# Attention with one key head: values' products of two key steps in one stretch

## The chip, the cores and the metric

The kernel runs on one core of one Trainium2 chip. The metric is the device time of one execution in microseconds. The engines are PE (TensorE, matmul; its weight loads are shown apart as PEld), DVE (VectorE), ACT (ScalarE), POOL (GpSimd) and SP (SyncE, which here only issues DMAs). Matmul results go to PSUM, which the kernel uses as eight banks of 128 x 512 float32; ACT and DVE empty them.

## The reference

The input x is 2048 rows of 448. Two layers of the same shape follow each other, with the same weights:

```
x = x + A(layernorm(x))     # 16 query heads of 28, one key head and one value head
x = x + B(layernorm(x))     # h = sigmoid(x w_gate) * (x w_up), 1792 wide; h w_down
```

In A, q = x wq, k = x wk and v = x wv. For each head the scores q k^T / sqrt(28) go through a softmax over all 2048 keys, the result is multiplied with v, and the heads side by side are multiplied with wo. All heads share k and v. The inputs and outputs are float32.

## The kernel before, in words

**Tiling.** A layer has 16 *units* (`u`): 128 query rows with all 16 heads, as four groups of four heads. Each unit has 16 *steps* (`kt`) of 128 keys; a layer has 256 steps. In one step the kernel does for its 128 keys:

- four score matmuls `s` (line 584), one for each group of heads: keys as weights (96 x 128, three parts of the split key under each other), 512 query columns; each fills one PSUM bank, and ACT writes its exponential to a tile `P` (line 587), 128 x 512 float32;
- the values' products `pv` (lines 591 to 595): four matmuls, each with the values of these keys as 128 x 32 weights on its own 32 columns of the array (`tile_position=(0, 32 * g)`), from the four `P`; they are added up over the 16 steps in one bank of their own. A float32 matmul shows as two records, so a step's group shows as eight;
- the row maxima of a later unit, `mx` (line 549): four matmuls of 32 x 128 weights, each on its own 32 rows of the array, into four banks; DVE reduces each one (line 554). The softmax needs the maxima before the scores of that unit start. They go through a transpose `mt` (line 575), a copy on DVE and a DMA issued by POOL (line 578) into row 28 of the unit's queries `QS`;
- a share of *filler*: matmuls that belong to other work. This is the query projection `qp`, the output projection `wo`, and for every two units the gated layer: seven times gate `gp` and up `up` (44 matmuls of 256 columns each time, chains of line 352), then `dn` (line 784). ACT and DVE make `th` and `h` between them (lines 746 to 758).

**Order.** The kernel is scheduled by hand: each engine does its instructions in the order in which the code records them. In every step a string of letters sets this order:

```
ORDER = "FSFSFSFSPXM"
```

S is one score matmul with its exponential, F one slice of filler, P the values' products of the step before, M one step of maxima (four matmuls, four reductions), X the bookkeeping: `tick()` runs the side stages of finished units (DMAs of the sums, reciprocal, output, layer norm, transposes), each due a number of ticks after the one before. The first 48 steps of the second layer use another string (`LATER`) in steps after a step with maxima. `fill.slice(ns)` lets the filler generators run until their estimated cost has used up `ns`; `rate` spreads what is left over the steps that remain. At the start of a slice, `flush()` records the instructions on ACT and DVE that were put off since the last one.

**Banks and buffers.** One PSUM bank holds `pv`. The seven others share one tag `f`: scores, maxima, and the filler's results. A new tile takes a bank that was given back earlier, and PE waits until its last reader is done. `P` tiles rotate in 8 buffers of 2 KB a partition.

Of the kernel before, what the change touches and what calls it, by code (L numbers as in the profile page):

```python
# [8 lines left out]
F32 = mybir.dt.float32  # L9
# [10 lines left out]
def interleaved_layers_kernel(ctx: ExitStack, tc: tile.TileContext, x, wq, wk, wv, wo, wg, wu, wd, out, layers=2):  # L20
# [6 lines left out]
    nc = tc.nc  # L27
    _, S, D = x.shape
    F = wg.shape[1]
    H, Dh = 16, 28  # L30
    NT, NB, G, KT, FC = S // 128, S // 512, H // 4, S // 128, F // 128
# [10 lines left out]
    wk1 = ctx.enter_context(tc.tile_pool(name="wk1", bufs=2))  # L42
# [27 lines left out]
    def flush(every=False):  # L70
        todo, pend[:] = pend[:], []
        for i, (due, fn) in enumerate(todo):
            if due > now[0] and not every:
                pend.append((due, fn))
            else:
                fn()
        if every and pend:
            flush(True)
# [89 lines left out]
    def prep_b():  # L168

        NPG, FIRST = 7, 8  # L170
        mall = wk1.tile([128, 3, NPG], F32, name="mall", bufs=1)
# [43 lines left out]
        def pieces(a, z, ahead):  # L215
            for n in range(a, z):
                r = get()
                squares(mall[:, n // NPG, n % NPG:n % NPG + 1], r, r)
                fetch(min(ahead, z - n - 1))
                yield  # L220
        yield from pieces(0, FIRST, 5)
        parts = wk1.tile([128, 2], F32, name="parto", bufs=1)
# [14 lines left out]

        yield from pieces(FIRST, 3 * NPG, 4)
        todo += [(columns, f) for f in range(FC)] + [(rows, f) for f in range(0, FC, 2)]
# [125 lines left out]
    def layer_tiles(l):  # L365
        KK[l] = lay.tile([128, 2, S], F16, tag="KK", name="KK")
        VV[l] = lay.tile([128, KT, 32], F32, tag="VV", name="VV")
        nc.vector.memset(VV[l][:, :, 28:32], 0.0)
        nc.vector.memset(VV[l][:, :, 28:29], 1.0)
# [55 lines left out]
    def qgen(l, b):  # L425

        XT = XTQ.pop((l, b))
        for g in range(G):
            yield from qproj(l, XT, b, g)
        flush(True)  # L430
# [7 lines left out]
    def load_qs(l, u):  # L438
        b, t = divmod(u, 4)
        assert QDONE[l, b] == G  # L440
        q = wk1.tile([96, G, 4, 128], F16, name="QS", bufs=2)
        QS[l, u] = q
        for i, part in ((0, 0), (1, 0), (2, 1)):
            for g in range(G):
                nc.sync.dma_start(q[32 * i:32 * i + 32, g],
                                  qd[l % 2][b, g, part, :, t * 128:(t + 1) * 128].rearrange("(h d) n -> d h n", d=32))
# [38 lines left out]
    def soon(u, kz):  # L485

        return (u == 0 or u in AHEAD) and kz <= S - 512
# [93 lines left out]
    def scores(l, u, kt, g, P):  # L581
        assert ("m", l, u) in stored, (l, u, kt)
        s = psf.tile([128, 512], F32, tag=BANKS["s"], name="s", bufs=NBK[BANKS["s"]])
        nc.tensor.matmul(s, KK[l][0:96, 0, kt * 128:(kt + 1) * 128], QS[l, u][:, g].rearrange("p h n -> p (h n)"),  # L584
                         start=True, stop=True)
        p = wk1.tile([128, 512], F32, tag="P", name="P", bufs=8)
        nc.scalar.activation(p, s, AF.Exp, scale=esc)  # L587
        P.append(p)

    def pv(l, u, kt, P):  # L590
        if kt == 0:
            PVS[l, u] = psv.tile([128, 512], F32, tag="v", name="pv")
        v = PVS[l, u]
        for g in range(4):
            nc.tensor.matmul(v[32 * g:32 * g + 32], VV[l][:, kt], P[g], start=kt == 0, stop=kt == KT - 1,  # L595
                             tile_position=(0, 32 * g))
        if kt == KT - 1:
            o = wk1.tile([128, 512], F32, name="pvs", bufs=1)
            nc.scalar.copy(o, v)
            PVS[l, u] = o  # L600
# [5 lines left out]
    def later(*stages):  # L606

        side.append([stages[0][0], list(stages)])
# [276 lines left out]
    fill = Filler()  # L885
# [7 lines left out]
    xr0 = {}  # L893

    def load_x0(i, eng=nc.sync):
        if i < HB:
            xr0[i] = wk1.tile([128, D], F32, tag="h", name="xr0", bufs=HB)
        else:
            xr0[i] = wk1.tile([128, D], F32, tag="P", name="xr0", bufs=8)
        eng.dma_start(xr0[i], x[0, i * 128:(i + 1) * 128])  # L900

    hl0, ls0 = {}, {}
    for i in range(NT):
        load_x0(i)
        if i == 1:
            load4(rkv[:, 0], wk)
            load4(rkv[:, 1], wv, nc.gpsimd)
        if i == 3:
            load4(rq, wq)
# [127 lines left out]
    ORDER = "FSFSFSFSPXM"  # L1037
    MORE = (10,)
    HEAD = U * KT - 32
    sparse = ()  # L1040
    LATER = "FSFSFSPFSXM"
    FIRST = KT * TB + 17
    KEEP = 28000
    VS = 1800
    for l in range(layers):
        mx = mxs[l]
        final = l + 1 == layers
        while late:
            late.pop(0)[1]()
        if not l:  # L1050
            mx.step()
            fill.slice(0.4 * QCH)
            mx.step()
        else:
            mx.todo.sort()
            n = sum(a[0] < 4 for a in mx.todo) + 2
            sparse = [i * (3 * KT - 1) // n for i in range(n)]
        if not final:
            layer_tiles(l + 1)
        if l:  # L1060
            for b in range(2, NB):
                fill.add(qgen(l, b), G * QCH)
        flush(True)
        fill.slice((0.75 if l else 0.4) * QCH)
        prevP = None
        rate = 0.0
        for step in range(U * KT):
            u, kt = divmod(step, KT)
            if step == HEAD and not final:
                mxs[l + 1] = Maxima(l + 1)  # L1070
            P = []
            for o in LATER if l and step < 3 * KT and step - 1 in sparse else ORDER:
                if o == "S":
                    scores(l, u, kt, len(P), P)
                elif o == "M":
                    if l and step < 3 * KT:
                        n = step in sparse
                    else:
                        n = 1 + (u == 0 and kt in MORE)
                    if not n:  # L1080
                        mx.visit()
                    for _ in range(n):
                        if not mx.step() and not final and l + 1 in mxs:
                            a = mxs[l + 1].between()
                            if a and soon(a[0], mxs[l + 1].need(a)):
                                mxs[l + 1].step(a)
                    if kt == 5 and u + 1 < U:
                        load_qs(l, u + 1)
                elif o == "P":
                    if prevP is not None:  # L1090
                        pv(*prevP)
                elif o == "X":
                    if u and kt == 1:
                        b = (u - 1) // TB
                        if (l, b) not in BLK:
                            BLK[l, b] = Block(l, b)
                        later(*BLK[l, b].tile(u - 1))
                    if l == 0:
                        paced(step)
                    tick()  # L1100
                    fed = sum(BLK[l, b].fed == TB for b in range(NBL) if (l, b) in BLK)
                    if fed < NBL - 1:
                        rate = fill.left / max(FIRST + TB * KT * fed - step, 1)
                    else:
                        rate = max(fill.left - KEEP, 0) / (U * KT - step)
                else:
                    fill.slice(rate / ORDER.count("F"))
            prevP = (l, u, kt, P)
        pv(*prevP)
        flush(True)  # L1110
        later(*BLK[l, NBL - 1].tile(U - 1))
        n = 0
        nx = None if final else mxs[l + 1]
        while side or pend or (fill.gens if final else not nx.started()):
            tick()
            for _ in range(0 if fine else 4):
                fill.slice(VS / 4)
            n += 1
            a = None if final else nx.between()
            if a:  # L1120
                kz = nx.need(a)
                if soon(a[0], kz):
                    go = n >= 2 and not fine
                elif kz == S - 128:
                    go = len(fine) > 1
                else:
                    go = True
                if go:
                    nx.step(a)
                    n = 0  # L1130
            for _ in range(2 if fine else 0):
                fill.slice(VS / 4)
        if not final:
            fill.slice(QCH)
# [21 lines left out]
```

## Time and profile before

| | us |
|---|---|
| median of three runs | 2310.68 |
| lowest, highest | 2307.3, 2311.08 |
| the profiled execution's own time | 2311.88 |
| its span | 2310.1 |
| PE busy | 2237.5 (97%) |
| DVE busy | 1640.6 (71%) |
| ACT busy | 1584.3 (69%) |
| POOL busy | 336.9 (15%) |

The first scores of layer 0's fifth unit start at 321.4 us and its last at 1129.0; layer 1 has its scores from 1247.4 to 2215.0, from its fourth unit on from 1381.7. A row of the grouped view names the line, the engine, the operation, the tiles (output<-inputs) and their shapes, the count, and then the busy time, the mean duration in ns, and the idle time of the engine just before with what ended it. A row of the stretches gives begin and end, the length, and the busy time with the count for PE, PEld, DVE, ACT and POOL, then PE's granted clock, the share of the DMA engines, and GB/s. A row of the timeline gives the start and the length from the first start to the last end, the engine, the line, and the count of equal instructions in a row. The ends of matmuls are modelled, so distances are taken from start to start. A row of the waits names who waited for whom, the time in all, the times and the longest.

### The profile page before, as it was taken

Reading aid. Unit: us, or ns where it says so; the run is one execution under the profiler, and the core shown is the slowest. Engines: PE = TensorE matmul, PEld = TensorE weight load, DVE = VectorE, ACT = ScalarE, POOL = GpSimd, SP = SyncE. Lnnn points to the kernel's source line nnn. Section 1 sums busy time; section 2 is a strip of 40 time slices with the busy share of each in tenths; the row PEclk is TensorE's granted clock in tenths of the full one; section 3 lists DMA queues with packets and bytes.
Section 4 is the critical chain, followed back from the end, with each engine's and each line's share of the span. In section 5 each row is a group of like instructions: output and inputs, shape, how many; then the busy total and the mean of one; then the engine's idle time right before and its main releaser. Section 6 shows DMA issues by size and latency. Waiting matters only on the chain.

```text
span 2310.1 us, 41518 instructions
## 1 busy us (share of the span) xinstructions
PE 2237.5 (97%) x15915; PEld 1011.2 (44%) x15915; DVE 1640.6 (71%) x2905; ACT 1584.3 (69%) x2595; POOL 336.9 (15%) x590
## 2 busy tenths in 40 slices
PE   7998999999999999999998999999999999999999
PEld 3322343444444444444563224444444444444456
DVE  7888887777777777777885447777777777777322
ACT  5797786677767677776514997777676767767731
POOL 5014771101110110101001010000000000000010
PEclk9999999999999999999999999999999999999999
DMA  4333661423313132332341123233232313233233
GB/s 137 105 101 96 205 218 41 110 74 96 114 55 105 43 111 71 96 103 74 106 133 38 31 59 106 69 91 91 83 89 54 105 42 108 65 91 88 76 100 116
DMA packets 203623, 213.28 MB, mean 92 GB/s; under 512 B 135377, under 2 KB 164241, under 8 KB 203425
## 3 DMA queue, kind: packets, MB, share of 16 engines
q1 hardware_dynamic: 198080, 195.78, 28.8%
q0 software_dynamic: 5344, 14.87, 1.8%
q8 instruction: 124, 2.03, 0.4%
q14 instruction: 75, 0.61, 0.1%
HBM read 175.37 MB, written 23.59 MB: 86 GB/s over the span
## 4 chain that ended last, share of the span: by engine, by line
PE 58%; DVE 3%; ACT 2%; DMA 1%; issue 1%; POOL 0%; SPq 0%; DVEq 0%; ACTq 0%; POOLq 0%
PE pv L595 13%; PE s L584 12%; PE dn L784 8%; PE up L352 8%; PE gp L352 8%; PE mx L549 4%; PE wo L695 2%; DVE mp L554 2%; ACT P L587 1%; PE qp L352 1%; DMA wgu<-wgu_d 1%; DVE th L754 0%; DMA XT<-hl 0%; DVE oT L676 0%; PE kv L352 0%
## 5 line engine op out<-in xcount | busy, mean ns | idle before, releaser
L587 ACT ACTIVATE P<-s,esc 128x512 f32<-128x512 f32 x2048 | 1323.8, 690 | 447.4 <-PE s L584 420.5
L554 DVE TENSOR_REDUCE mp<-mx 128x1 f32<-128x512 f32 x2048 | 1269.7, 683 | 426.3 <-PE mx L549 424.1
L584 PE MATMUL s<-QS,KK 96*128 96x512 f16 x2048 | 764.2, 382 | 39.2 <-DVE mp L554 15.0
L352 PEld LDWEIGHTS <-wgu 128*128 128x128 f16 x4928 | 458.2, 97 | 237.8 <-issue 93.9
L595 PE MATMUL pv<-P,VV 128*32 128x512 f32 x4096 | 548.2, 607 | 0.0
L352 PE MATMUL gp<-XT,wgu 128*128 128x256 f16 x2464 | 374.4, 273 | 0.1
L352 PE MATMUL up<-XT,wgu 128*128 128x256 f16 x2464 | 373.9, 273 | 0.4 <-ACT P L587 0.3
L784 PE MATMUL dn<-WD,h 128*128 128x448 f16 x1344 | 321.4, 352 | 0.0
L584 PEld LDWEIGHTS <-KK 96*128 96x128 f16 x2048 | 197.4, 97 | 155.9 <-issue 59.8
L549 PEld LDWEIGHTS <-QH 32*128 32x128 f16 x1792 | 45.8, 91 | 350.4 <-issue 347.9
L549 PE MATMUL mx<-KK,QH 32*128 32x512 f16 x1792 | 186.5, 386 | 6.1 <-ACT P L587 3.1
L784 PEld LDWEIGHTS <-h 128*128 128x128 f16 x1344 | 123.8, 97 | 137.4 <-issue 25.7
L595 PEld LDWEIGHTS pv<-P,VV 128*32 128x32 f32 x4096 | 81.0, 108 | 199.6 <-issue 196.5
L757 ACT ACTIVATE h<-th 128x512 f16<-128x512 f32 x112 | 70.3, 628 | 110.1 <-DVE th L754 109.8
L669 POOL TENSOR_TENSOR lb<-pvs,lb 128x512 f32<-128x512 f32 x32 | 41.4, 1294 | 604.8 <-DMA lb<-sums 499.2
L306 POOL TENSOR_SCALAR rs<-mv 128x1 f32<-128x1 f32 (+1 forms) x50 | 12.1, 241 | 781.7 <-DVE mv L291 738.2
L352 PE MATMUL qp<-XT,WQ 128*128 128x512 f16 x352 | 115.9, 387 | 0.7 <-ACT P L587 0.4
L754 DVE SCALAR_TENSOR_TENSOR th<-th,up 128x512 f32<-128x512 f32 x112 | 76.1, 680 | 38.8 <-PE up L352 32.2
L758 DVE SCALAR_TENSOR_TENSOR h<-th,h 128x512 f16<-128x512 f32 x112 | 77.6, 693 | 36.0 <-ACT h L757 36.0
L746 ACT ACTIVATE th<-gp,gsc 128x512 f32<-128x512 f32 x112 | 76.7, 685 | 37.8 <-PE gp L352 37.8
L695 PE MATMUL wo<-WO,oT 128*128 128x448 f16 x384 | 95.1, 359 | 5.0 <-ACT oT L675 4.6
L352 PEld LDWEIGHTS <-WQ 128*128 128x128 f16 x352 | 33.4, 98 | 59.8 <-issue 34.2
(151 smaller groups left out, 916.9 us busy)
## 6 DMA issues: line engine op xcount, KB each, us to landing
wgu<-wgu_d SPq DMA_DIRECT2D x224, 512.0 KB
QS<-qd SPq DMA_DIRECT2D x384, 32.0 KB
lb<-sums SPq DMA_DIRECT2D x128, 64.0 KB
xr<-in_A_x_dram SPq DMA_DIRECT2D x32, 224.0 KB
qd<-qst POOLq DMA_DIRECT2D x28, 256.0 KB, 2.7
wgu_d<-sgu POOLq DMA_DIRECT2D x14, 512.0 KB, 4.1
x2d<-x SPq DMA_DIRECT2D x16, 224.0 KB
xr<-x2d SPq DMA_DIRECT2D x16, 224.0 KB
```

The source lines that it names most:

```text
L352: nc.tensor.matmul(ps, a, b, start=n == 0, stop=n == 10)
L549: nc.tensor.matmul(ps[h][:, i * w:(i + 1) * w], qh[32 * h:32 * h + 32, g], KK[l][32 * h:32 * h + 32, 1, ka:kz], start=True, stop=True, til ...
L554: nc.vector.tensor_reduce(o, ps[h].rearrange("p (g k) -> p g k", g=n), axis=AX.X, op=OP.max)
L584: nc.tensor.matmul(s, KK[l][0:96, 0, kt * 128:(kt + 1) * 128], QS[l, u][:, g].rearrange("p h n -> p (h n)"), start=True, stop=True)
L587: nc.scalar.activation(p, s, AF.Exp, scale=esc)
L595: nc.tensor.matmul(v[32 * g:32 * g + 32], VV[l][:, kt], P[g], start=kt == 0, stop=kt == KT - 1, tile_position=(0, 32 * g))
L695: nc.tensor.matmul(p, v["oT"][:, a, h * 128:(h + 1) * 128], WO[:, c, h], start=n == 0, stop=n == 11)
L746: defer(lambda: nc.scalar.activation(th, gp.rearrange("p j n -> p (j n)"), AF.Tanh, scale=gsc))
L754: nc.vector.scalar_tensor_tensor(t, th, 1.0, up.rearrange("p j n -> p (j n)"), op0=OP.add, op1=OP.mult)
L757: nc.scalar.activation(h[:, 0], t, AF.Copy, scale=2.0 ** -17)
L758: defer(lambda: nc.vector.scalar_tensor_tensor(h[:, 1], t, 2.0 ** -17, h[:, 0], op0=OP.mult, op1=OP.subtract), 1)
L784: nc.tensor.matmul(p, hs[f // 2][:, a, o:o + 128], WD[:, f, c], start=n == 0, stop=n == 3 * FC - 1)
```

## The change

In layer 0 from the fifth unit (`u > 3`) and in layer 1 from the fourth (`u > 2`), 400 of the 512 steps, a step's order depends on whether its number in the unit is even or odd. An even step has two letters P at its end, an odd step has none, and each P now takes one waiting step: so an even step does the values' products of the last two steps, one group right after the other. The odd step has its first two scores together, the even step its last two. Per pair of steps there are seven slices of filler instead of eight, and the share of a slice is set accordingly. X stands earlier in both strings. Before these units the order is as it was; `LATER` only concerns the first three units of layer 1, so it stays in use there.

`P` has 12 buffers instead of 8, and the first load of x, which uses the same tag, names the same number. The descriptor scratch that the program sets aside for DMAs issued by POOL is set to 8192 bytes a partition, which makes room for the four buffers.

```diff
-        p = wk1.tile([128, 512], F32, tag="P", name="P", bufs=8)
+        p = wk1.tile([128, 512], F32, tag="P", name="P", bufs=12)
...
+    PAIR = ("FSFSXFSSPPM", "FSSFSXFSFM")
...
-        prevP = None
+        waiting = []
...
-            for o in LATER if l and step < 3 * KT and step - 1 in sparse else ORDER:
+            paired = (l or u > 3) and u > 2
+            if paired:
+                order = PAIR[kt % 2]
+            else:
+                order = LATER if l and step < 3 * KT and step - 1 in sparse else ORDER
+            for o in order:
...
                 elif o == "P":
-                    if prevP is not None:
-                        pv(*prevP)
+                    for _ in range(len(waiting) if not paired else min(1, len(waiting))):
+                        pv(*waiting.pop(0))
...
-                    fill.slice(rate / ORDER.count("F"))
-            prevP = (l, u, kt, P)
-        pv(*prevP)
+                    fill.slice(2 * rate / (PAIR[0] + PAIR[1]).count("F") if paired else rate / ORDER.count("F"))
+            waiting.append((l, u, kt, P))
+        while waiting:
+            pv(*waiting.pop(0))
...
-    nc = _bacc.Bacc("TRN2", target_bir_lowering=False, num_devices=1)
+    nc = _bacc.Bacc("TRN2", target_bir_lowering=False, num_devices=1, dynamic_dma_scratch_size=8192)
```

PE at the end of a step in layer 1, before (the `x4` are four products, eight records of the profile):

```order
L584 LDWEIGHTS KK
L584 MATMUL s<-QS,KK 128x512
L595 MATMUL pv<-P,VV 32x512 x4
L549 LDWEIGHTS QH
L549 MATMUL mx<-KK,QH 128x512
```

The same place of an even step in the changed kernel:

```order
L584 LDWEIGHTS KK
L584 MATMUL s<-QS,KK 128x512
L584 LDWEIGHTS KK
L584 MATMUL s<-QS,KK 128x512
L595 MATMUL pv<-P,VV 32x512 x8
L549 LDWEIGHTS QH
L549 MATMUL mx<-KK,QH 128x512
```

Two scores stand together, and two groups of products follow without anything between. In the whole program the products stand in 312 stretches instead of 511.

PE at the end of an odd step in layer 1 in the changed kernel, where the filler is the up projection (of each kind of matmul one with its weight load):

```order
L584 LDWEIGHTS KK
L584 MATMUL s<-QS,KK 128x512
L352 LDWEIGHTS wgu
L352 MATMUL up<-XT_18534,wgu 128x256
L549 LDWEIGHTS QH
L549 MATMUL mx<-KK,QH 128x512
```

Where the products stood, there is now a slice of filler, and the maxima follow it. That is so in 225 places of the program instead of 58.

ACT in layer 1 in the changed kernel, through the exponentials of an even step (first four rows), of the odd step behind it (the next four exponentials) and the next even step's first:

```order
L587 ACTIVATE P_19444<-s_19442,esc_100 128x512
L587 ACTIVATE P_19452<-s_19450,esc_100 128x512
L587 ACTIVATE P_19462<-s_19460,esc_100 128x512
L587 ACTIVATE P_19466<-s_19464,esc_100 128x512
L587 ACTIVATE P_19495<-s_19493,esc_100 128x512
L587 ACTIVATE P_19499<-s_19497,esc_100 128x512
L746 ACTIVATE th_19501<-gp_19415,gsc_101 128x512
L587 ACTIVATE P_19510<-s_19508,esc_100 128x512
L587 ACTIVATE P_19519<-s_19517,esc_100 128x512
L587 ACTIVATE P_19543<-s_19541,esc_100 128x512
```

The tanh of the gate, recorded at the start of the odd step's second slice, stands between the second and the third exponential of that step. In the 200 odd steps this place holds another ACT instruction 33 times, the place between the third and the fourth 62 times.

More of the change, by code (lines that the diff above doesn't have):

```diff
@@ L898, in load_x0 @@
         else:
-            xr0[i] = wk1.tile([128, D], F32, tag="P", name="xr0", bufs=8)
+            xr0[i] = wk1.tile([128, D], F32, tag="P", name="xr0", bufs=12)
         eng.dma_start(xr0[i], x[0, i * 128:(i + 1) * 128])
```

## The prediction

> **What bounds the kernel now.** I read the page first (busy shares and slices), then the two stretches that the change touches, then the waits of PE in them, then the timeline of single steps.
>
> ```profile
> PE 2237.5 (97%) x15915; PEld 1011.2 (44%) x15915; DVE 1640.6 (71%) x2905; ACT 1584.3 (69%) x2595; POOL 336.9 (15%) x590
> PE   7998999999999999999998999999999999999999
> PE pv L595 13%; PE s L584 12%; PE dn L784 8%; PE up L352 8%; PE gp L352 8%; PE mx L549 4%; PE wo L695 2%; DVE mp L554 2%; ACT P L587 1%; PE qp L352 1%; DMA wgu<-wgu_d 1%; DVE th L754 0%; DMA XT<-hl 0%; DVE oT L676 0%; PE kv L352 0%
> L587 ACT ACTIVATE P<-s,esc 128x512 f32<-128x512 f32 x2048 | 1323.8, 690 | 447.4 <-PE s L584 420.5
> L595 PE MATMUL pv<-P,VV 128*32 128x512 f32 x4096 | 548.2, 607 | 0.0
> 321.40:1129.00 807.60, 792.38 (x5769) 363.86 (x5766) 608.56 (x1067) 574.84 (x922) 101.91 (x215) 1.00 0.30 87
> 1381.70:2150.00 768.30, 762.64 (x5509) 347.50 (x5507) 567.02 (x968) 551.19 (x870) 55.78 (x121) 1.00 0.28 82
> ```
>
> The last two rows are layer 0 from its fifth unit and layer 1 from its fourth: PE is busy for 792.38 of 807.60 us and 762.64 of 768.30 us, at a granted clock of 1.00. ACT and DVE have a quarter free, and what they miss is mostly PE's output. So what shortens PE's own row shortens the run, unless a new wait of PE eats it. PE's waits there are small today:
>
> ```profile
> PE s L584 <- DVE mp L554: 2.1, 6, 0.5
> PE s L584 <- ACT P L587: 2.1, 5, 0.4
> PE wo L695 <- ACT P L587: 0.5, 1, 0.5
> ...
> PE s L584 <- ACT P L587: 7.7, 9, 3.1
> PE s L584 <- DVE mp L554: 3.4, 13, 0.5
> PE mx L549 <- ACT P L587: 3.1, 4, 0.9
> ```
>
> The first three rows are layer 1, the others layer 0: 4.7 and 14.2 us, together 18.9, of waits for a PSUM bank that ACT (exponentials) or DVE (maxima) still reads.
>
> **What a stretch of values' products costs beside its arithmetic.** Start times on PE in one step:
>
> ```profile
> 1507.84 0.38 PE L584 MATMUL s<-QS,KK 96*128 96x512 f16 x1
> 1508.15 1.06 PE L595 MATMUL pv<-P,VV 128*32 128x512 f32 x8
> 1509.15 0.39 PE L549 MATMUL mx<-KK,QH 32*128 32x512 f16 x4
> 1509.47 0.55 PE L784 MATMUL dn<-WD,h 128*128 128x448 f16 x2
> 1509.86 0.38 PE L584 MATMUL s<-QS,KK 96*128 96x512 f16 x1
> 1510.08 0.73 PE L784 MATMUL dn<-WD,h 128*128 128x448 f16 x3
> 1510.65 0.38 PE L584 MATMUL s<-QS,KK 96*128 96x512 f16 x1
> ```
>
> A score ahead of dn takes 0.22 us (1509.86 to 1510.08), ahead of pv 0.31: entering pv costs 0.09. From pv to mx it is 1.00 us. The trace has one place where two pv groups already stand together, at the end of layer 1:
>
> ```profile
> 2215.03 0.38 PE L584 MATMUL s<-QS,KK 96*128 96x512 f16 x1
> 2215.34 1.92 PE L595 MATMUL pv<-P,VV 128*32 128x512 f32 x16
> 2217.20 0.61 PE L352 MATMUL gp<-XT,wgu 128*128 128x256 f16 x4
> ```
>
> Sixteen records take 1.86 us where two times eight take 2.00: a joint stretch saves 0.14 beside one entry of 0.09.
>
> The loss is that the odd step's maxima no longer follow pv but filler. At the layer change they do so already:
>
> ```profile
> 1151.98 3.77 PE L784 MATMUL dn<-WD,h 128*128 128x448 f16 x19
> 1155.69 0.39 PE L549 MATMUL mx<-KK,QHB 32*128 32x512 f16 x4
> ```
>
> Nineteen dn at 0.19 each (0.57 for three above) are 3.61, and mx starts after 3.71: entering mx from filler costs 0.10.
>
> **The sum of the sure part.** Counted in the two orders: 199 stretches of pv fewer, 167 entries into mx from other work than pv more, and in 11 pairs the transpose mt, which followed pv, now follows filler.
>
> ```profile
> 1503.73 1.06 PE L595 MATMUL pv<-P,VV 128*32 128x512 f32 x8
> ...
> 1504.61 0.22 PE L575 MATMUL mt<-id,m 128*16 128x128 f16 x1
> ```
>
> There pv took 0.88 instead of 1.00, so those 11 lose 0.12 and, at pv's price, an entry of 0.09. 199 x (0.09 + 0.14) = 45.8; less 167 x 0.10 = 16.7; less 11 x 0.21 = 2.3: PE's row gets **26.8 us** shorter. The number of matmuls is the same, and filler moves only between slots: seven slices a pair instead of eight.
>
> **What the new order may cost.** Each tile of scores or maxima takes the bank of an earlier one, and the odd step is now short. I lay it out for the gate and up phase, where steps are shortest.
>
> ```profile
> 1464.06 0.38 PE L584 MATMUL s<-QS,KK 96*128 96x512 f16 x1
> 1464.48 2.66 ACT L587 ACTIVATE P<-s,esc 128x512 f32<-128x512 f32 x4 [1.10 <-PE s L584]
> 1467.34 0.40 PE L549 MATMUL mx<-KK,QH 32*128 32x512 f16 x4
> 1467.76 2.48 DVE L554 TENSOR_REDUCE mp<-mx 128x1 f32<-128x512 f32 x4 [0.97 <-PE mx L549]
> 1468.34 0.60 PE L352 MATMUL gp<-XT,wgu 128*128 128x256 f16 x4
> 1468.60 0.69 ACT L587 ACTIVATE P<-s,esc 128x512 f32<-128x512 f32 x1 [1.45 <-PE s L584]
> 1468.77 0.38 PE L584 MATMUL s<-QS,KK 96*128 96x512 f16 x1
> 1469.18 0.62 ACT L757 ACTIVATE h<-th 128x512 f16<-128x512 f32 x1
> 1469.70 1.26 ACT L587 ACTIVATE P<-s,esc 128x512 f32<-128x512 f32 x2
> ...
> 1567.36 2.42 ACT L587 ACTIVATE P<-s,esc 128x512 f32<-128x512 f32 x4
> ```
>
> ACT and DVE start 0.42 after the score or the maxima. Exponentials in a row come every 0.58 ((2.42 - 0.69) / 3), an ACT instruction between two adds 0.52 (1469.18 to 1469.70), and the reductions come every 0.60 ((2.48 - 0.68) / 3). A slice of filler is four matmuls in 0.43 today (1468.34 to 1468.77) or three; with seven slots for the same work I take 0.46. In an odd step, counted from its first score: third score 0.90, fourth 1.58, maxima 2.36 (0.10 of entry in it), next even step's first score 3.15 (0.33 of maxima, 0.46 of filler later). The four exponentials end at 1.11, 1.69, 2.27, 2.85. In the order the fourth maxima tile takes the third score's bank in 107 of 200 odd steps: margin 0.09. The next first score takes the fourth's in 77: margin 0.30. With nothing between, no wait.
>
> With something between: in 33 odd steps an ACT instruction (tanh, h, a copy) stands between second and third exponential, and the maxima wait 0.52 - 0.09 = 0.43 in 107/200 of them, else the next score 0.22 in 77/200: 33 x 0.27 = 9 us. In 62 it stands between third and fourth: 62 x 0.22 x 0.39 = 5 us. On DVE the even step's reductions are over 0.75 before the odd step's begin (between the two maxima lie 0.33 of maxima, 0.46 of filler and 2.36, together 3.15; less 4 x 0.60). In 68 odd steps two or more instructions stand between, which makes the next four about 0.45 late; a later score that takes a maxima bank then waits some 0.13 on average: 9 us. New waits: 23 us. Against that the place of today's bank waits goes: the second score of an odd step took a bank of the maxima just before it in a third of the pairs, now in an eighth; I take half of today's 18.9 off, 10 us. **Net 13 us.** Bounds: from below, no new wait and 10 gone (-10); from above, every one of the 107 tight maxima waiting the 0.43 (46 us), with the other 14 (60 us), and none of today's gone. The rows have slack left in the bare step, so I stay near the lower third.
>
> **What I cost at nothing.** P has twelve buffers because three steps of four are alive; the first buffer is asked for again one step after its pv, so ACT's write is covered. The side stages come earlier in a step, and their ticks are alternately longer and shorter; POOL's product and ACT's cast are the pair that could block ACT:
>
> ```profile
> L675 ACT CAST oT<-lb 128x512 f16<-128x512 f32 x32 | 19.7, 616 | 8.4 <-POOL lb L669 8.4
> ...
> 1505.40 0.62 POOL L578 DMA_DIRECT2D QS<-mr  x1 [8.63 <-DVE mr L577]
> ...
> DMA to landing us min/median/max: 1.6/2.1/5.2
> ```
>
> The cast waits 8.4 us in all today, and its tick gets the longer half. The row of maxima for the next unit is issued at 1505.40, 4.46 us ahead of that unit's first score (1509.86), and lands in 2.1: of 2.3 us to spare the short odd step takes about 0.5. If the smaller descriptor scratch held POOL's transfers back, this is where it would show; 25 units at up to 0.5 us, 12 us, is its upper end. I take zero.
>
> **The sum.** The profiled execution took 2311.9 us (span 2310.1). 2311.9 - 26.8 + 13 = 2298; it lies 1.2 above the median of the runs, so I predict **2297 us**. Its own range is 2288 to 2308.
>
> **Rivals.**
> - *The whole gain arrives.* If the waits stay at today's level: 2310.7 - 26.8 = 2284 (2279 to 2288). For it: the bare odd step has no wait by the rows, and the even step leaves ACT and DVE two us of pv to catch up. Against: margins of 0.09 and 0.30 below one ACT instruction.
> - *The odd step's banks decide (slower).* If the fourth maxima and the scores behind them wait on average 0.20 us a pair more than today, that is 200 x 0.20 = 40: 2310.7 - 26.8 + 40 = 2324. It decides from 0.13 us a pair on (26.8 / 200). For it: ACT needs 2.85 of 3.15 us there; a backlog brought in from the even step hits every pair. Against: the order puts two scores first, and both engines idle a quarter. The Trainium skill, "TensorEngine Tiling (Array Packing)", PSUM Bottleneck, warns that packing speeds TensorE up but not the emptying of PSUM; today's 18.9 us of such waits agree in kind, not in size.
> - *The seam is not free.* If the second group pays its head again in mid-kernel, the 0.14 and so 199 x 0.14 = 27.9 us go: 2310.7 + 1.1 + 13 = 2325. Against it stands the row of sixteen, but that is one place. The Trainium skill, "TensorE: Matmul & The Clock Gate", The mechanism, says that a weight load overlaps running matmuls only where the row group differs, which would make this the outcome; the row of 1.86 disagrees.
>
> **How the numbers follow.** Forecast 0.50, whole gain 0.26, banks 0.16, seam 0.05, something else 0.03. From no change a measurement can tell about 0.2%, 4.6 us. Faster by more: the whole gain and nine tenths of the forecast, 0.72. Slower by more: most of banks and seam, 0.16. Within: 0.12. For eight in ten I leave out the ends of the whole gain below 2280 and of the slower cases above 2318.
>
> **What would show it.** pv in stretches of sixteen with 1.86 us to the next start; filler to mx 0.10; PE busy time about 27 us less. The waits of PE on ACT and DVE should sum to about 32 us in the two stretches, with mx on ACT the new row. If mx and s wait over 45 us, I am wrong on the price of the odd step; if the pv stretch takes 2.00, on the seam; if a unit's first score waits for the maxima's row, on the scratch.

## The result, and the profile after

| us | before | changed |
|---|---|---|
| median | 2310.88 (4 runs, 2307.3 to 2311.99) | 2288.85 (4 runs, 2284.06 to 2289.33) |
| profiled execution, span | 2311.88, 2310.1 | 2284.06, 2282.3 |

The ratio is 0.9904 (95% interval 0.9888 to 0.992): 22 us faster. The time lies in the predicted range, and 8 us under the predicted 2297. The profiled execution of the changed kernel is the lowest of its four runs; the same kernel measured a second time (below) gave 0.9922 (0.9909 to 0.9935).

From the page of the changed kernel, the engines, PE's slices and the three groups that the change touches on PE:

```profile
PE 2213.4 (97%) x15915; PEld 1030.0 (45%) x15915; DVE 1638.6 (72%) x2905; ACT 1545.7 (68%) x2595; POOL 338.1 (15%) x590
PE   8998999999999999999999999999999999999989
L584 PE MATMUL s<-QS,KK 96*128 96x512 f16 x2048 | 699.3, 380 | 29.7 <-DVE mp L554 12.0
L595 PE MATMUL pv<-P,VV 128*32 128x512 f32 x4096 | 506.0, 602 | 0.6 <-ACT pvs L599 0.6
L549 PE MATMUL mx<-KK,QH 32*128 32x512 f16 x1792 | 188.4, 385 | 3.3 <-DVE mp L554 2.2
```

The scores' row before:

```profile
L584 PE MATMUL s<-QS,KK 96*128 96x512 f16 x2048 | 764.2, 382 | 39.2 <-DVE mp L554 15.0 <-ACT P L587 14.8 <-DMA QS<-mr 4.1
```

PE is busy 24.1 us less with as many instructions, and the products' group fell from 548.2 to 506.0. The scores' group fell by more, but that is no gain by itself: two scores that stand together overlap in the modelled ends (0.60 for two in the timeline below, 0.38 for one), and 400 such neighbours make up the difference. Where the time went shows in the stretches. First before, then changed: layer 0 from its fifth unit, the change of layers, and layer 1 from its fourth unit to its last score:

```profile
321.40:1129.00 807.60, 792.38 (x5769) 363.86 (x5766) 608.56 (x1067) 574.84 (x922) 101.91 (x215) 1.00 0.30 87
1129.00:1247.40 118.40, 111.42 (x891) 68.56 (x888) 94.62 (x171) 26.09 (x49) 17.54 (x38) 1.00 0.38 111
1381.70:2215.00 833.30, 827.64 (x5957) 378.84 (x5956) 579.44 (x991) 600.83 (x950) 60.39 (x131) 1.00 0.28 82
```

```profile
316.80:1118.10 801.30, 787.51 (x5771) 372.99 (x5769) 605.46 (x1066) 555.73 (x922) 102.13 (x215) 1.00 0.31 88
1118.10:1233.70 115.60, 110.38 (x882) 68.35 (x881) 92.91 (x168) 26.00 (x49) 17.00 (x38) 1.00 0.37 110
1365.70:2186.60 820.90, 816.40 (x5961) 390.56 (x5960) 580.40 (x991) 583.24 (x950) 60.97 (x131) 1.00 0.29 84
```

The two stretches that the change touches are 6.3 and 12.4 us shorter, 18.7 together, and the change of layers 2.8. The rest, up to 27.8 between the two profiled spans, is the first 320 us (4.6), layer 1's first three units (2.2) and the end (0.6 longer), where nothing is changed but buffers and scratch. That rest is chance: the first stretch took 316.8 here, 320.1 when the change was run again, and 316.8 in a kernel without joint stretches. The granted clock goes with it. Layer 1's first three units, before and then changed:

```profile
1247.40:1381.70 134.30, 129.66 (x751) 34.95 (x752) 64.49 (x114) 121.27 (x203) 14.59 (x28) 0.97 0.14 39
1233.70:1365.70 132.00, 127.35 (x756) 34.93 (x757) 67.22 (x118) 119.97 (x203) 15.26 (x29) 1.00 0.15 41
```

The clock is 0.97 before and 1.00 here; when the change was run again it was 0.97, and these units took 134.3 us once more. In the first stretch as many instructions (1924 or 1925) keep PE busy for 289.8 us before, 286.4 here and 290.7 in the second run, at 0.97, 0.98 and 0.97.

One pair of steps in the changed kernel, start times on PE:

```profile
1502.26 0.60 PE L584 MATMUL s<-QS,KK 96*128 96x512 f16 x2
1502.79 1.92 PE L595 MATMUL pv<-P,VV 128*32 128x512 f32 x16
1504.64 0.39 PE L549 MATMUL mx<-KK,QH 32*128 32x512 f16 x4
...
1507.28 0.60 PE L352 MATMUL up<-XT,wgu 128*128 128x256 f16 x4
1507.81 0.39 PE L549 MATMUL mx<-KK,QH 32*128 32x512 f16 x4
```

Sixteen records of the products take 1.85 us to the next start (1502.79 to 1504.64; 1.857 as the median in both layers). Four `up` take 0.53 to the maxima, 0.44 of arithmetic and 0.09 to 0.10 of entry.

The waits of PE, layer 0's stretch (first four rows) and layer 1's, each row with its sum, its count and its longest:

```profile
PE kv L352 <- ACT P L587: 3.2, 1, 3.2
PE s L584 <- ACT P L587: 2.9, 10, 0.5
PE s L584 <- DVE mp L554: 2.5, 8, 0.5
PE kv L352 <- DVE mp L554: 2.4, 8, 0.4
...
PE s L584 <- DVE mp L554: 1.9, 5, 0.4
PE gp L352 <- ACT P L587: 0.6, 1, 0.6
PE s L584 <- ACT P L587: 0.5, 3, 0.2
```

With their small rows these are 12.6 and 3.5 us, 16.1. Before has 14.5 and 5.2 in the same two stretches, 19.7 (the prediction's 18.9 is of slightly shorter ones). So by this view the waits fell, and no row of maxima on ACT came. Yet 27 us of PE's row should be gone and only 18.7 are. The view hides part of it: it takes a wait from the modelled end of a matmul, and a start that is late by less than the model's tail (0.38 long, 0.22 to the next start) shows as busy time. I therefore count **late starts**: for each kind of neighbours on PE (score after up, fourth maxima after third, ...) the distance from start to start, less the 5% quantile of that kind over all runs, summed over the starts that are more than 20 ns late; distances inside a group of products are left out. It gives 25.2 us before and 31.1 changed in layer 0's stretch, 12.6 and 15.5 in layer 1's: 37.8 to 46.6. So PE's own row is 18.7 + 8.8 = 27.5 us shorter, and 8.8 of it are lost to more waiting.

### The profile page after: what moved, and what is told of

The parts are those of the page before. It is cut to its first block, busy times and chain, and to the rows that moved or that the text cites. A ratio compares the mean times of both kernels' runs of the same rounds, so it can differ in the third digit from the quotient of the medians.

```text
span 2282.3 us, 41511 instructions
## 1 busy us (share of the span) xinstructions
PE 2213.4 (97%) x15915; PEld 1030.0 (45%) x15915; DVE 1638.6 (72%) x2905; ACT 1545.7 (68%) x2595; POOL 338.1 (15%) x590
## 4 chain that ended last, share of the span: by engine, by line
PE 59%; DVE 6%; ACT 3%; DMA 1%; issue 1%; SPq 0%; POOL 0%; ACTq 0%; DVEq 0%; POOLq 0%
PE pv L595 14%; PE s L584 13%; PE dn L784 9%; PE up L352 8%; PE gp L352 7%; PE mx L549 4%; DVE mp L554 4%; PE wo L695 2%; ACT P L587 2%; PE qp L352 1%; ACT h L757 0%; DVE th L754 0%; DMA rc<-sums 0%; DVE h L758 0%; DMA XT<-hl 0%
## 5 line engine op out<-in xcount | busy, mean ns | idle before, releaser
L587 ACT ACTIVATE P<-s,esc 128x512 f32<-128x512 f32 x2048 | 1291.4, 689 | 477.1 <-PE s L584 462.1
L584 PE MATMUL s<-QS,KK 96*128 96x512 f16 x2048 | 699.3, 380 | 29.7 <-DVE mp L554 12.0
L595 PE MATMUL pv<-P,VV 128*32 128x512 f32 x4096 | 506.0, 602 | 0.6 <-ACT pvs L599 0.6
L352 PE MATMUL gp<-XT,wgu 128*128 128x256 f16 x2464 | 364.7, 273 | 0.7 <-ACT P L587 0.6
L352 PE MATMUL up<-XT,wgu 128*128 128x256 f16 x2464 | 362.4, 273 | 0.8 <-DVE mp L554 0.4
L784 PE MATMUL dn<-WD,h 128*128 128x448 f16 x1344 | 314.4, 353 | 0.0
L595 PEld LDWEIGHTS pv<-P,VV 128*32 128x32 f32 x4096 | 101.3, 109 | 263.6 <-issue 259.9
L549 PE MATMUL mx<-KK,QH 32*128 32x512 f16 x1792 | 188.4, 385 | 3.3 <-DVE mp L554 2.2
```

The costliest lines, as they stand in the source:

```text
L352: nc.tensor.matmul(ps, a, b, start=n == 0, stop=n == 10)
L549: nc.tensor.matmul(ps[h][:, i * w:(i + 1) * w], qh[32 * h:32 * h + 32, g], KK[l][32 * h:32 * h + 32, 1, ka:kz], start=True, stop=True, til ...
L784: nc.tensor.matmul(p, hs[f // 2][:, a, o:o + 128], WD[:, f, c], start=n == 0, stop=n == 3 * FC - 1)
```

## The experiments

All ratios are to the kernel before, timed on the same chip. "Late" is the sum of late starts in the two stretches.

**Room alone.** The changed kernel with its buffers and scratch, but the old order everywhere.

```diff
-            paired = (l or u > 3) and u > 2
+            paired = False
```

> Twelve P buffers and the smaller descriptor scratch alone; order of all steps as before. Theory 1 (the gain is PE's own row: fewer entries into the products, no seam): as before, 2311 within 3 us. Theory 2 (the gain comes from the order of the letters, which keeps banks from being waited for): also as before. Theory 3 (four more buffers relieve ACT, or the memory layout, and the joint stretch is incidental): 10 us or more faster. If the first 320 us get shorter here too, the 4.6 us that the changed kernel won ahead of its first paired step belong to the buffers.

2310.4 us, 1.0006 (0.9998 to 1.0015); stretches 806.4 and 833.3, late 36.6. Twelve buffers and the smaller scratch are worth nothing here, in either direction. The first stretch took 316.8 here too, which by the expectation would give the 4.6 us to the buffers; but the change run again, with the same buffers, took 320.1.

**The seam cut.** The change, with the two groups of products parted by one score.

```diff
-    PAIR = ("FSFSXFSSPPM", "FSSFSXFSFM")
+    PAIR = ("FSFSXFSPSPM", "FSSFSXFSFM")
```

> The changed kernel with the even step's last score put between its two groups of products (F S F S X F S P S P M), all else equal: same buffers, same odd step, both groups still in the even step. Theory 1: each of 200 pairs pays an entry (0.09) and a leaving (0.14) again, 46 us, so 2289 + 46 = 2335, slower than before by about 1%, because the odd step's maxima still pay 0.10 for following filler. Theory 2 (order and waits): within 5 us of the changed kernel, 2284 to 2294.

2334.24 us, 1.0111 (1.0098 to 1.0124), 45 us above the change. The sum had 200 x (0.09 + 0.14) = 46. What a stretch of products costs beside its arithmetic is shown by this run: the only edit is the place of one score, and late starts are even 3.8 fewer (42.8).

**Plain order.** Joint stretches, but scores and filler in turn and X before M, as the old string had them: the odd step's fourth score stands right ahead of the maxima.

```diff
-    PAIR = ("FSFSXFSSPPM", "FSSFSXFSFM")
+    PAIR = ("FSFSFSFSPPXM", "FSFSFSFSXM")
```

> Products of two steps together in the even step, but the letters otherwise as before: even F S F S F S F S P P X M, odd F S F S F S F S X M. Theory 1: the same entries and seams are saved, so 2289 plus what waits for banks come; the page would show PE's waits on ACT and DVE. If the own order matters little: 2285 to 2295. If it is what keeps the banks apart (theory 2): 2305 or more, with the odd step's maxima or the scores behind them waiting for ACT.

2324.03 us, 1.0063 (1.005 to 1.0076): slower than before, with the same seam saved. Late is 76.6, of which 26.2 at the odd step's fourth maxima and 10.9 at its third. This is the rival "the odd step's banks decide", and its price: late starts are 38.8 us over before, where the rival had 40. One place in this run's timeline:

```profile
1435.83 0.69 ACT L587 ACTIVATE P<-s,esc 128x512 f32<-128x512 f32 x1
1436.01 0.38 PE L584 MATMUL s<-QS,KK 96*128 96x512 f16 x1
1436.32 0.64 PE L549 MATMUL mx<-KK,QH 32*128 32x512 f16 x3
1436.42 0.68 ACT L746 ACTIVATE th<-gp,gsc 128x512 f32<-128x512 f32 x1
1437.15 0.37 PE L549 MATMUL mx<-KK,QH 32*128 32x512 f16 x1 [0.19 <-ACT th L746]
```

Four maxima that start within 10 ns elsewhere are torn apart: the fourth starts 0.57 us after the third (three alone would last 0.39, and last 0.64, so the third is 0.25 late itself), and the view books 0.19 of it to ACT. The rest sits in PE's busy time, as the group's row in this run shows: 212.2 us, 188.4 in the change.

```profile
L549 PE MATMUL mx<-KK,QH 32*128 32x512 f16 x1792 | 212.2, 386 | 9.6 <-ACT P L587 3.4 <-DVE mp L554 2.2 <-DVE th L754 1.5
```

**X late.** The change with X back ahead of M.

```diff
-    PAIR = ("FSFSXFSSPPM", "FSSFSXFSFM")
+    PAIR = ("FSFSFSSPPXM", "FSSFSFSFXM")
```

> The changed kernel with X moved back to just ahead of M in both strings. In the changed kernel PE waits 6 us in layer 0 ahead of kv (a side stage that X now issues between a score and a slice), which it did not before. If the early X is the cause: kv's waits go and the run is 3 to 6 us shorter, 2283 to 2286. If the waits belong to the shorter odd step: same as the changed kernel, 2287 to 2291, with the waits at another tile.

2298.26 us, 0.9951 (0.9938 to 0.9964), 9 us longer than the change; I had expected 3 to 6 shorter, or no difference. The key and value matmuls (`kv`) no longer wait behind a score (8.2 to 0.7 us), but scores and maxima wait more: late 53.5. The change of layers is back at 119.0.

**Order alone.** The change's two strings, but each step does its own group of products.

```diff
-    PAIR = ("FSFSXFSSPPM", "FSSFSXFSFM")
+    PAIR = ("FSFSXFSSPM", "FSSFSXFSFPM")
```

> The changed kernel's letters and seven slices, but each step does one group of products again: even F S F S X F S S P M, odd F S S F S X F S F P M. Theory 1 (the joint stretch pays, the own order only has to keep the banks apart): the 26.8 us come back, less the waits that the own order saves, 2308 to 2316. Theory 2 (the own order is itself worth 10 us or more, as plain letters with the joint stretch cost 13 us against before): 2295 to 2303.

2294.58 us, 0.9948 (0.9935 to 0.9961): 12.7 us faster without any joint stretch, at the lower edge of what theory 2 gave. Late falls to 27.5, 10.3 under before. The stretches take 801.3 and 828.3: in layer 0 just what the whole change takes, in layer 1 7.4 more. So over order alone the joint stretches bring 7.4 us, about their 26.8 less the 19.1 of late starts that come with them.

**Pairs from layer 0's third unit on and in all of layer 1.**

```diff
-            paired = (l or u > 3) and u > 2
+            paired = l or u > 1
```

> Pairs also in the third and fourth unit of layer 0 and the first three of layer 1 (80 steps more, 40 pairs). Theory 1: entry and seam are saved, 0.23 a pair, and in layer 1 most of these steps have no maxima that would pay 0.10: 7 to 9 us less, 2280 to 2282. Rival: these units are held by ACT and DVE (ACT is busy 91% in layer 1's first three units), so PE's saving turns into waits: 2286 to 2292.

2293.88 us, 0.9947 (0.9935 to 0.9958), no faster than the change: the 7 to 9 us did not come, and the rival's 2286 to 2292 was just missed. Up to the fifth unit it takes 328.0 us (the change run again 320.1), and layer 1's first three units 135.4 (134.3). The granted clock was a little lower as well, 0.96 in both places against 0.97 there, so a part of it may be that. The gain of the seam is not had in these units. Why is not shown. The rival's reason, that ACT and DVE hold them, fits two rows: ACT is busy for 118.85 of the 135.4 us in layer 1's, and short reductions, below, shorten layer 0's first units by 15 us.

**X first.** X two places earlier in both strings.

```diff
-    PAIR = ("FSFSXFSSPPM", "FSSFSXFSFM")
+    PAIR = ("FSXFSFSSPPM", "FSSXFSFSFM")
```

> X one place earlier still in both strings: F S X F S F S S P P M and F S S X F S F S F M. With X late the run was 9 us longer than the changed kernel, 5 of them in layer 0's pairs and 4 at the layer change. If earlier is better throughout: 2 to 5 us less than the changed kernel. If what counts is that the side stages' instructions on ACT and DVE do not fall between the scores that the maxima wait for: same or up to 5 us longer.

2297.72 us, 0.9956 (0.9944 to 0.9969), 6.6 us over the change run again, where the second theory had up to 5; late 56.5. What came over the change stands at the even step's first score in layer 0 (9.4, the change 2.3) and the odd step's fourth maxima (11.2 in both layers, the change 4.4).

**The change again.**

> The changed kernel once more on this chip, as the measure for the other three: 2285 to 2290, with the stretch of layer 1 from its fourth unit within 1 us of 820.9 and layer 0's within 2 us of 801.3. The first 320 us should show whether the 4.6 us of the first profile were chance.

2291.17 us, 0.9922 (0.9909 to 0.9935), a little over the 2285 to 2290 expected; stretches 801.4 and 821.2, late 46.9, change of layers 115.7, and 320.1 for the first four units. The stretches repeat within 0.3 us, the start does not.

**The odd step's third score later, X in the middle.** Two more orders.

```diff
-    PAIR = ("FSFSXFSSPPM", "FSSFSXFSFM")
+    PAIR = ("FSFSXFSSPPM", "FSSFXFSSFM")
```

> The changed kernel with the odd step's third score one slice of filler later and together with the fourth (odd string FSSFXFSSFM; even string unchanged). Theory: the place of the scores is a compromise; the third exponential and the fourth now end later (the fourth about 0.2 to 0.3 us), the maxima after one slice wait for them, as in the run with plain order but less: 4 to 10 us longer than the change, 2293 to 2299. Rival: the waits at the third score come from the even step's reductions, and a slice more lets them go: 4 to 8 us shorter, 2281 to 2285.

```diff
-    PAIR = ("FSFSXFSSPPM", "FSSFSXFSFM")
+    PAIR = ("FSFSFXSSPPM", "FSSFSFXSFM")
```

> The changed kernel with X one slice later in both strings (FSFSFXSSPPM, FSSFSFXSFM), so that a side stage's matmul follows filler and not a score. Theory A: what X costs where it stands in the change is the bank that key and value matmuls of the second layer take right behind a score (8 us of layer 0's waits stand between a score and such a matmul); these go and little comes: 4 to 8 us shorter than the change, 2281 to 2285. Theory B: X's distance ahead of the maxima counts, as in the run with X back at its old place (9 us longer): between the two, 2291 to 2298.

2299.99 us, 0.9968 (0.9955 to 0.9981), and 2303.39 us, 0.9985 (0.9975 to 0.9995). With the third score later, 26.0 us fall on the odd step's fourth maxima and 15.7 on the next first score; the theory had the direction but too small a size (late is 59.6, 13 more than the change, and the ratios differ by 11 to 15 us). With X in the middle late is 59.9, more than with X at either end; that it would lie between them was wrong. 16.0 of it is the odd step's second score, 8.8 its fourth maxima, and `kv` still costs 7.6. Of the orders tried, the change's waits least among those with joint stretches.

**Short reductions.** The changed kernel, then the kernel before, with DVE's reductions over half of each bank. Half of the keys is left out of the row maxima, so nothing bounds the exponent for the others; these two are probes, not replacements.

```diff
-                nc.vector.tensor_reduce(o, ps[h].rearrange("p (g k) -> p g k", g=n), axis=AX.X, op=OP.max)
+                nc.vector.tensor_reduce(o, ps[h].rearrange("p (g k) -> p g k", g=n)[:, :, :w // 2], axis=AX.X, op=OP.max)
```

> The changed kernel, with the reductions of the maxima reading only the first half of each bank's keys (half of the keys is left out of the row maxima; everything else is computed as before). A reduction then takes about 0.35 us instead of 0.60. Theory: of the some 46 us that PE loses between starts in the two stretches of the changed kernel, a part of DVE's own (reductions that come late because other instructions stand between) is about a third to a half, so 12 to 20 us go: 2269 to 2277. Rival: ACT's exponentials come last almost everywhere and DVE is only named because it ends near them: under 5 us go, 2284 or more.

> The kernel before, with the reductions of the maxima reading only the first half of each bank's keys (half of the keys is left out of the row maxima). It stands beside the changed kernel with the same reductions, whose two stretches took 791.4 and 814.9 us. Theory: the change's new waits hang on DVE, so with short reductions more of its 26.8 us arrives than the 18.7 that arrived with whole ones: the two stretches together 23 to 27 us longer than 1606.3, so 1629 to 1633, and the whole run 2270 to 2277. Rival: short reductions take as much off the old order's waits, and the difference stays at 17 to 20 us: 1623 to 1626, the run 2265 to 2269.

The change: 2247.79 us, 0.9747 (0.9733 to 0.9762). The kernel before: 2260.16, 0.9795 (0.9778 to 0.9812). The reductions' row of the change with short reductions:

```profile
L554 DVE TENSOR_REDUCE mp<-mx 128x1 f32<-128x256 f32 x2048 | 724.8, 417 | 742.7 <-PE mx L549 740.8
```

Its two stretches:

```profile
301.80:1093.20 791.40, 780.22 (x5771) 372.97 (x5770) 407.16 (x1067) 553.21 (x922) 103.64 (x215) 1.00 0.31 89
1338.80:2153.60 814.80, 811.65 (x5961) 390.62 (x5960) 383.58 (x991) 580.92 (x950) 60.87 (x131) 1.00 0.29 84
```

The same two stretches of the old order with short reductions:

```profile
299.20:1091.40 792.20, 787.70 (x5769) 363.11 (x5766) 405.98 (x1067) 576.26 (x922) 101.78 (x215) 1.00 0.31 89
1338.90:2161.60 822.70, 822.16 (x5957) 378.88 (x5956) 380.46 (x991) 604.29 (x950) 60.34 (x131) 1.00 0.28 84
```

A reduction takes 0.42 us instead of 0.68. In the change the stretches lose 16.0 us, inside the 12 to 20 expected; the whole run lost more than that and lies under the 2269 to 2277, since the first four units, which I had left out, take 15 us less (301.8): there the reductions' length counts as well. In the old order the two stretches come to 1614.9 us, where the theory had 1629 to 1633 and the rival 1623 to 1626. Both fell. With short reductions the old order waits almost nowhere (late 11.1; PE is busy for 822.16 of 822.70 us), and the whole change is worth 8.7 us in the stretches instead of 18.7. PE's row still gets 28.0 us shorter (8.7 and 19.3 more of late starts). So the late starts that the change has in excess are not those of long reductions. Places, both stretches together:

| late starts, us | before | order alone | change | change, short red. | before, short red. |
|---|---|---|---|---|---|
| odd step, first and second score | 15.7 | 5.6 | 3.1 | 0.0 | 3.6 |
| even step, third and fourth score | 8.1 | 5.4 | 4.9 | 0.9 | 4.5 |
| even step, first score | 1.3 | 0.4 | 5.3 | 6.1 | 0.0 |
| even step, second score | 0.2 | 0.3 | 10.3 | 7.0 | 0.0 |
| odd step, fourth maxima | 3.7 | 0.0 | 4.4 | 4.6 | 0.5 |
| `kv` | 0.2 | 5.0 | 8.2 | 8.9 | 0.7 |
| all others | 8.6 | 10.8 | 10.4 | 2.9 | 1.8 |
| sum | 37.8 | 27.5 | 46.6 | 30.4 | 11.1 |

One wait near 400 us (last section) stands at an even step's fourth score in the two kernels with the old order (3.3 of the 8.1, and as much of the 4.5) and in `kv` in the other three (2.9 to 3.4). Apart from it, the first two rows are what short reductions cure, and what the new order cures too: before to order alone, they fall by 9.5. Against order alone, the next three came with the joint stretches, and when the reductions are short 17.7 of their 20.0 us stay. The rest of `kv` goes with X's place.

Why short reductions don't help at the second score shows in the changed kernel's timeline, at one of its regular places:

```profile
1577.81 0.68 DVE L754 SCALAR_TENSOR_TENSOR th<-th,up 128x512 f32<-128x512 f32 x1
1578.32 0.40 PE L549 MATMUL mx<-KK,QH 32*128 32x512 f16 x4
1578.52 0.63 ACT L757 ACTIVATE h<-th 128x512 f16<-128x512 f32 x1 [0.44 <-DVE th L754]
1579.18 0.69 DVE L758 SCALAR_TENSOR_TENSOR h<-th,h 128x512 f16<-128x512 f32 x1 [0.70 <-ACT h L757]
1579.21 0.38 PE L584 MATMUL s<-QS,KK 96*128 96x512 f16 x1
1579.79 2.48 DVE L554 TENSOR_REDUCE mp<-mx 128x1 f32<-128x512 f32 x4
1580.53 0.38 PE L584 MATMUL s<-QS,KK 96*128 96x512 f16 x1 [0.37 <-DVE mp L554]
```

The odd step's maxima are written at 1578.32, and their reductions start 1.47 us later instead of 0.42, because DVE stands 0.70 us for ACT's `h` with the reductions queued behind it. The even step's second score takes the first maxima's bank in 73 of 200 pairs, and here starts 0.53 late. In 16 pairs such a wait on a maxima's bank sums to 6.0 of the 10.3 us. In 14 of the 16, with 5.7 us, the trace has DVE standing for an ACT instruction ahead of the reductions: nine times for `h` (4.9 us), four times for `oT` and once for a scaled weight. Of the other 4.3 us at the second score, 3.1 are waits for banks of scores, that is for exponentials, and 1.1 for a bank of `up`. These instructions were not moved to try it, so the handing between DVE and ACT is read from the trace and not tested.

## Why the prediction was right, and where it was not

- **The sure part, 26.8 us:** 27.5 came by the stretches and the late starts; the same sum over order alone gives 26.5, and with short reductions 28.0. Entry, seam, entry of maxima and their counts all hold: 1.857 us for sixteen records, 0.10 from filler to maxima, and 45 us lost when the seam is cut. So the rival "the seam is not free" is refuted in mid-kernel too.
- **Net 13 us of new waits:** 8.8 by late starts, and part of the nearness is luck. The prediction priced new waits at three kinds of places with 23. These places got 14.8 more than before: 4.0 at the next first score, 10.1 at the second score, 0.7 at the fourth maxima. Gone at the odd step's first two scores and the even step's last two are 12.5, where it had 10 (both without the one wait that moved to `kv`). `kv` got 4.6 beside that wait, which was costed at nothing, and others gave 1.8 more. So the term that failed is the 23: it was 8.2 too high, and 6.4 of waits that were not in the sum hide most of that. The 10 was a guess at half of the view's 18.9, and there were twice as many late starts as the view showed.
- **The three parts of the 23** were sized as 9, 5 and 9. The fourth maxima's 9 was mis-sized: 4.4, of which 3.7 stood there before. I had multiplied "ACT has an instruction behind the second exponential" (33; the trace has 36) with "the fourth maxima takes the third score's bank" (107 of 200) as if they were independent; counted together in the order they meet in 11 steps, not 18. The odd step itself was laid out nearly right: in steps of gate and up alone, the maxima start 2.39 us after its first score instead of 2.36 and the next first score 3.27 instead of 3.15; over all odd steps, with longer filler, it is 2.50 and 3.41. The first three exponentials ended where I had them (1.11, 1.68, 2.26); the fourth has its median at 3.07 instead of 2.85, since in many steps an ACT instruction stands between. The next first score's 5 is 5.3, 1.3 of them there before. DVE's 9 has its counterpart at the second score, 6.0 of the 10.3, but mostly by DVE's standing for ACT and not, as laid out, by more instructions of its own.
- **Order and joint stretches:** the order alone lowers late starts by 10.3, which is most of the 11.3 us that its two stretches gain. The joint stretches then bring 7.4 of their 26.8. In the prediction's terms these were 10, which was a guess, and 3.8 (26.8 less 23).
- **X at nothing:** wrong both ways. X behind a score brings `kv` late (4.8 in all beside the moved wait of 3.4), and the change of layers took 114.7 to 115.9 us with X at the change's place or earlier, and 118.3 to 119.4 with X a slice later or at its old place (runs with whole reductions). Its cause was not looked for; X's place in the order is what these kernels have in common.
- **Buffers and scratch at nothing:** right, 1.0006.
- **The banks rival** was real but not for this order: the plain order pays it and ends slower than before. The term "waits over 45 us" in my list of signs was no use, since the view of waits shows about half of them or less (19.7 of 37.8, 16.1 of 46.6); the maxima's group and distances from start to start show it.
- **The sum for the median:** predicted 2297, measured 2289, which is the edge between the forecast and the rival "the whole gain arrives"; its waits did not stay at today's level, so it is not that rival. Late starts account for 4.2 of the 8, PE's row for 0.7, the change of layers for 2.8.

## What to carry to other kernels

Where PE sets the time, the entry into a differently tiled matmul and the seam between its groups have a price that can be read from start-to-start distances; multiplied by the counts, it came out here to within 1 us. Whether the gain arrives is decided by the order of what stands between: an order of its own was worth 12.7 us without the joint stretches, and with joint stretches in the plain order the run was 15 us slower than before. A view of waits that works from modelled ends can miss half of the waiting, so late starts should be counted by place, and how often two conditions meet should be counted in the order, not multiplied. A few us between two profiled executions in a stretch that nobody changed can be the granted clock: look at it before looking for a cause.

## What the runs showed of the hardware

In layer 0, near 400 us, PE stands once for 3.1 to 3.2 us in both kernels: ACT's cast `hl` (line 321) waits for DVE's `xn` (line 329), with exponentials queued behind. In the changed kernel, the stretches around it:

```profile
399.30:403.10 3.80, 0.60 (x2) 0.17 (x3) 1.35 (x5) 1.18 (x3) 0.00 (x0) 0.67 0.36 64
403.10:408.00 4.90, 4.87 (x34) 1.44 (x33) 2.60 (x6) 2.70 (x6) 0.00 (x0) 0.56 0.87 287
408.00:412.00 4.00, 4.00 (x38) 2.63 (x35) 2.81 (x5) 2.42 (x4) 1.27 (x1) 1.00 0.28 61
```

The timeline there:

```profile
401.92 0.56 ACT L321 CAST hl<-xn 128x448 f16<-128x448 f32 x1 [2.70 <-DVE xn L329]
403.13 0.67 PE L352 MATMUL kv<-WKV,XT 128*128 128x56 f16 x11 [3.23 <-ACT P L587]
404.86 3.19 PE L595 MATMUL pv<-P,VV 128*32 128x512 f32 x16
```

The granted clock is 0.56 in the 4.9 us after the pause, and sixteen records of the products take 3.19 us instead of 1.92. So here some 2 us more were lost behind the pause (an estimate, 44% of 4.9). In the kernel before it is much the same: clock 0.65 from 410.4 to 415.0, after a wait of 3.14. But such a pause does not always do it. In the run with room alone, whose order is the old one, the same pause is as long:

```profile
405.88 0.38 PE L584 MATMUL s<-QS,KK 96*128 96x512 f16 x1 [3.21 <-ACT P L587]
406.19 1.06 PE L595 MATMUL pv<-P,VV 128*32 128x512 f32 x8
405.80:410.80 5.00, 4.81 (x44) 2.23 (x47) 5.00 (x10) 4.38 (x10) 0.00 (x0) 1.00 0.85 284
```

The clock stays at 1.00 in the 5 us behind it, and eight records take their 1.06 us. What decides between the two was not tested.
